# Block-sparse attention and a hard-swish MLP in one kernel: key windows stored as 64 own rows and the next 32, no zero fills, fewer TensorE instructions at the start, a new order

## The chip, the cores and the metric

The kernel runs on one core of a Trainium2 chip. The metric is the device time of one execution in microseconds (us): three runs before the change took 216.30, 216.91 and 217.49 us, so the median is 216.91 us. Engines are named as in the profile: PE (matrix products), DVE (vector), ACT (scalar), POOL (GpSimd, which here issues all loads), SP (which issues stores and small moves).

## The reference

Four batches, eight heads, 768 tokens, head size 64. Each query sees its neighbours at a distance below 16 and, besides, 24 block keys (the maximum over 32 keys each) with the mean of the block's values. The result goes through a two-layer MLP with 2048 hidden units.

```python
k_sum = k.reshape(B, H, nb, 32, D).max(axis=3)
v_sum = v.reshape(B, H, nb, 32, D).mean(axis=3)
mask_l = np.abs(pos[:, None] - pos[None, :]) < 16
scores_all = concat([where(mask_l, scale * q @ k.T, -1e9), scale * q @ k_sum.T + log(32)])
a = softmax(scores_all)
attn = a @ concat([v, v_sum])
h = x @ w_in                      # x: attn, 3072 tokens x 512
out = (h * clip(h + 3, 0, 6) / 6) @ w_out
```

## The kernel before

A tile of 64 queries (QB) needs 96 neighbouring keys (WIN = 64 + 2 x 16) and the 24 block keys, 120 rows in all (KEYS). There are 12 such tiles to a batch. The queries are shifted by 16 against the keys, so that the 96 keys are the 64 own rows of a key tile and 32 rows of a neighbouring one. `kaug[p]` holds the keys of a pair of heads in this form, `vaug[i]` the values of a batch (two buffers, used in turn), `qT` the transposed queries, `at[p]` the exponentials of the scores, `mask` the band.

Before, the 32 foreign rows are those of the tile *before*, and they stand in rows 0 to 31. They are filled by copies (`halo`, `third`) or by an extra load (`load_ahead`). Row 0 of `vaug` up to row 31 is also read by the products that sum values over blocks (`vsum_first`, `vsum`, with `ind` as a 0/1 matrix of 96 rows), and so these rows are first filled with zeros (`empty`, eight operations, one for each buffer and pair of heads).

Work goes in eight half batches s = 0..7 of 384 tokens. For batch 0 the steps are: `k_step` (keys transposed on PE, maximum over blocks on DVE, copies into `kaug`), `q_step` and `q_wide` (queries), `scores`, `vsum_first`, `values_first` (first half, one pair of heads at a time: products, reciprocal, scaling, transposition, copy into x) and `values`. Batches 1 to 3 use `turn`, `scores4`, `vsum`, `values`. Then the MLP: `f1(s, ft)` makes 128 of the 2048 hidden units for 384 tokens (four products of 384 columns, then `relu` on ACT and `gate` on DVE), `f2(s, ts, part)` a quarter of the sum for 128 tokens (four products of 512 columns), and the last quarter is followed by a copy and a store.

The order of everything is written out by hand as a table, `ORDER`: `Plan.issue` takes its tokens from left to right and emits each operation to its engine, and each engine works strictly in that order. `k2.0` is step 0 of `k_step(2)`; `s021` is scores of batch 0, pair 2, half 1; `v01` is `values_first(1)`; `v411` is `values(0, 1, 1)`; `F0x3` is `f1(0, 3)`; `G02x0` is `f2(0, 2, ...)` from column 0. The letter after a colon (A, D) picks ACT or DVE. Loads: `K`, `Q`, `V` for keys, queries, values; `I` and `O` for the two weights; `Q0w` and `Q1w` for rows of queries. Tokens that begin with `~ - _ =` emit products of a tile of ones (`keep`, L774), whose result is never read: `~n` is n products of 512 columns, `-n` of 128, `_n` of 64, `=n` one of n x 64. They stand in front, where PE would else wait for loads.

PSUM has three banks `h`, one `o`, and two pairs `S`; `f1` uses the `h` banks, so three of its results at most wait for ACT and DVE at a time.

Of the kernel before, what the change touches and what calls it, by code (L numbers as in the profile page):

```python
# [9 lines left out]
F32 = mybir.dt.float32  # L10
BF16 = mybir.dt.bfloat16
AF = mybir.ActivationFunctionType
# [17 lines left out]
c.0 K00.0 c.7 c.17 c.6 c.8:A K01.0 c.10:D c.5 c.1 _40 -15 k0.0 k0.2:A c.18 ~1 =2 k1.0 K02.0 ~12 =3 k2.0 k3.0 c.15:D c.2 c.3  # L30
s000.0 k0.3:A c.13:D c.4 c.11:A k1.1 Q00.0 q0.0 k1.4 k0.1 c.20 k1.2:A Q01.0 ~2 =5 q1.0 k0.4 k1.3:D c.9:A c.14:A c.19 k2.3:A
q0.1:A s000.1 q0.2:A =1 s010.0 s010.1 k2.2:A k3.2:D k3.3:D k3.1 V00.0 h000.0:D h001.0:D k2.1 k2.4 s000.2 ~2 =5 v00.0 V01.0 u0.0
h010.0:D s020.0 c.16 s010.2 q1.2:A u0.3:D u0.1:D u0.4:D v01.0 v01.1 v01.2 v00.1 q1.1:A V02.0 h020.0:A h021.0:A h011.0:A v00.2
s020.1 v01.3 v00.3 V03.0 u1.0 u1.3:A h030.0:D s030.0 k3.4 ~2 s030.1 u1.4:D v01.4 h031.0:D Q0w0.0 Q0w1.0 v01.5:D Q0w2.0 =1 q3.0
q3.1:D q2.0 u1.1:A u1.2:D s020.2 v02.0 v02.1 v02.2 s021.0 v02.3 s030.2 v03.0 v03.1 q2.1:A v03.2 s011.0 v03.3 v00.4 v00.5:D
v02.4 s021.1 s011.1 s021.2 v03.4 v03.5:D s011.2 v02.5:A s031.0 s031.1 s001.0 s031.2 I2.0 F0x3.0 F0x3.1 F0x3.2 F0x3.3 F0x3.4
F0x3.5 I4.0 F0x6.0 F0x6.1 F0x6.2 F0x4.0 F0x4.1 F0x4.2 F0x4.3 v411.0 v411.1 F0x5.0 F0x4.4 F0x4.5 v411.2 s001.1 I8.0 u0.2:A
s001.2 F0x8.0 F0x8.1 F0x8.2 F0x5.1 I0.0 F0x5.2 F0x11.0 F0x1.0 F0x11.1 F0x11.2 F0x1.1 F0x1.2 F0x1.3 F0x1.4 F0x1.5 v410.0 v410.1
F0x7.0 F0x7.1 F0x7.2 v410.2 F0x10.0 F0x10.1 I12.0 F0x13.0 F0x13.1 F0x15.0 F0x15.1 F0x13.2 F0x10.2 v411.3 v411.4:D v410.3
v410.4:A F0x15.2 F0x14.0 F0x14.1 F0x14.2 F0x9.0 F0x9.1 F0x9.2 F0x0.0 F0x0.1 F0x2.0 F0x2.1 K13.0 K10.0 c.12:A F0x0.2 K12.0 K11.0  # L40
w10.0 Q1w1.0 F1x14.0 F1x14.1 F1x14.2 F1x4.0 F1x4.1 F1x4.2 F1x2.0 F1x2.1 F1x2.2 w10.1:D F0x2.2 F0x2.3 F0x2.4 F0x12.0 F0x12.1
F0x12.2 F1x8.0 F1x8.1 F1x8.2 F1x1.0 F1x1.1 F1x1.2 F0x0.3 F0x0.4 F0x0.5 F0x2.5 F1x9.0 F1x9.1 F1x9.2 F1x5.0 F1x5.1 F1x5.2 F1x15.0
F1x15.1 w11.0 w11.2 F1x15.2 w11.3:D Q1w4.0 Q1w2.0 Q1w0.0 w10.2 w10.3:D q6.0 q6.1:A q7.0 q7.1:A F1x7.0 F1x7.1 w11.1:A F1x7.2
F1x12.0 F1x12.1 F1x12.2 O0.0 G02x0.0 Q1w5.0 Q1w3.0 q4.0 q4.1:A q5.0 q5.1:A F1x6.0 F1x6.1 F1x6.2 O1.0 G02x0.1 s100.0 s100.1
s100.3 F1x3.0 w12.0 F1x11.0 F1x11.1 w13.0 w13.2 F1x3.1 F1x11.2 w12.2 w12.1:D O2.0 G02x0.2 s101.0 s101.1 O3.0 F1x10.0 G02x0.3
G02x0.4:A w13.3:D w13.1:A s101.3 F1x0.0 G00x0.0 G00x0.1 w12.3:D s100.2 s101.2 s100.4 V10.0 h100.0:D F1x10.1 h110.0:A F1x10.2
F1x3.2 s110.0 s110.1 s110.2 s101.4 s110.3 G00x0.2 G00x0.3 G00x0.4:A V12.0 u4.0 h130.0:D h120.0:A F1x0.1 u4.1:D u4.2:A u4.4:D
u4.3:D u4.5:D G02x0.5 G01x0.0 G01x0.1 G01x0.2 s110.4 F1x0.2 h111.0:A v100.0 v100.1 v100.2 h121.0:A v101.0 v101.1 v101.2 G01x0.3
G01x0.4:A K20.0 K21.0 K22.0 K30.0 K23.0 w21.0 F1x13.0 F1x13.1 F1x13.2 v100.3 v100.4:A w20.0 w21.3 G12x0.0 w21.2:A v101.3
v101.4:A V22.0 H2.0 h101.0:A w20.3 G12x0.1 G12x0.2 F2x2.0 F2x2.1 F2x11.0 F2x2.2 F2x11.1 F2x11.2 s111.0 w23.0 s111.3 F2x1.0  # L50
F2x1.1 F2x1.2 F2x3.0 F2x3.1 F2x3.2 F2x15.0 F2x15.1 F2x15.2 Q22.0 w23.3 G12x0.3 s111.1 G12x0.4:A F2x5.0 F2x5.1 h131.0:A F2x5.2
F2x6.0 G10x0.0 s111.2 w22.0 w22.3 s111.4 w23.4:A V20.0 H2.1:A K33.0 F2x13.0 F2x13.1 F2x13.2 G10x0.1 F2x6.1 F2x0.0 F2x0.1 F2x0.2
u5.0 u5.1:A u5.5:A F2x6.2 v110.0 v111.0 v111.1 v111.2 Q30.0 F2x4.0 F2x4.1 F2x4.2 Q21.0 Q23.0 Q20.0 w22.4:A F2x10.0 F2x10.1
# [12 lines left out]
G30x0.2 F4x13.1 u6.3:A F4x13.2 w33.3 F4x7.0 F4x7.1 F4x7.2 G21x0.5 G20x0.5 v211.4 F4x6.0 F4x6.1 F4x6.2 v211.7 v211.6 v211.5
w30.1 F4x11.0 F4x11.1 F4x11.2 G30x0.3 G30x0.4:A G30x0.5 F4x1.0 F4x1.1 w33.2:A F4x1.2 w32.4:D F4x5.0 F4x5.1 F4x5.2 G22x0.5
s300.0 s300.3 s300.1 F4x3.0 F4x12.0 F4x12.1 F4x9.0 F4x3.1 F4x9.1 w31.5:A w33.4:A w33.1 w32.1 F4x9.2 F4x12.2 w32.5:D s300.2
G31x0.0 G31x0.1 G31x0.2 s300.4 F4x3.2 s310.0 s310.3 s310.4 s310.1 s310.2 F4x0.0 F4x0.1 F4x0.2 F4x10.0 G31x0.3 w30.5:A F4x10.1
w33.5:D F4x10.2 v301.0 v301.1 v300.0 v301.2 v300.1 G31x0.4:A G31x0.5 v300.2 v300.3 v301.3 F5x14.0 F5x14.1 v301.5 v301.7 v301.6  # L70
v301.4 F5x2.0 G42x0.0 G42x0.1 F5x1.0 F5x1.1 F5x2.1 G42x0.2 F5x14.2 F5x1.2 F5x2.2 s301.0 s301.3 G42x0.3 G42x0.4:D s301.1 s301.2
F5x6.0 F5x6.1 F5x6.2 F5x4.0 F5x4.1 F5x4.2 F5x3.0 s311.0 s311.3 s311.4 F5x9.0 F5x9.1 F5x9.2 F5x3.1 F5x3.2 s311.1 s311.2 s301.4
# [90 lines left out]
def kernel(  # L163
# [80 lines left out]
    def low(x):  # L244

        return (1 - x) * HQ
# [563 lines left out]
```

## Time and profile before

| what | value |
| --- | --- |
| median of three runs | 216.91 us |
| span of the profiled execution | 214.9 us (its own time outside the span isn't shown; the median of the runs is 2.0 us above it) |
| PE busy | 208.8 us, 97% of the span, 2564 products |
| DVE busy | 162.7 us, 76% |
| ACT busy | 135.9 us, 63% |
| loads and stores | 22.68 MB, mean 106 GB/s |
| share of the chain that ended last | PE 86%, POOL 5%, DMA 4% |

The page gives averages over a start, a long dense part and an end. The chain of waits is read for where each part is bound, the timeline of each engine for the start, and the table of windows for how full the engines are in each part.

### The profile page before, as it was taken

The page shows a single profiled execution, that of the slowest core. Times are in us where ns is not written, and L with a number is a line of the kernel's source. Part 1 is how long each engine was busy: PE and PEld are TensorE (multiplying, and loading weights), DVE is VectorE, ACT ScalarE, POOL GpSimd, SP SyncE. Part 2 cuts the span into 40 slices and gives each one's busy share as a digit, 9 for nine tenths or more (in the row PEclk, how much of TensorE's full clock was granted, in tenths as well). Part 3 has the DMA queues.
Part 4 walks back from the last instruction along what each step waited for, and adds up shares of the span by engine and source line. Part 5 has one row for each costly group of instructions (what it writes and reads, how often), then busy time and mean ns, then how long its engine had stood idle before and what let it go on. Part 6 is the DMA issues. An engine that isn't in the chain of part 4 may idle for free.

```text
span 214.9 us, 6125 instructions
## 1 busy us (share of the span) xinstructions
PE 208.8 (97%) x2564; PEld 119.7 (56%) x2564; DVE 162.7 (76%) x318; ACT 135.9 (63%) x264; POOL 49.5 (23%) x66
## 2 busy tenths in 40 slices
PE   7998999999999999999999999999999999999994
PEld 7566656555555565565555555555555555564443
DVE  6987999999899999898899889887865555550021
ACT  3987878887898988756578696566346355520110
POOL 7977358906643244000000000000000000000000
PEclk9999999999999999999999999999999999999999
DMA  5999999999999999930334234113314400113123
GB/s 75 159 155 189 203 188 170 190 203 162 206 160 187 181 135 151 108 146 11 38 37 143 28 37 110 49 21 39 70 19 81 78 0 3 49 49 122 52 80 139
DMA packets 91724, 22.68 MB, mean 106 GB/s; under 512 B 82224, under 2 KB 88752, under 8 KB 91696
## 3 DMA queue, kind: packets, MB, share of 16 engines
q0 software_dynamic: 62288, 14.41, 72.7%
q1 hardware_dynamic: 29264, 7.80, 15.4%
q8 instruction: 20, 0.33, 0.6%
q10 hardware_dynamic: 144, 0.07, 0.1%
q14 instruction: 8, 0.07, 0.1%
HBM read 28.82 MB, written 6.29 MB: 163 GB/s over the span
## 4 chain that ended last, share of the span: by engine, by line
PE 86%; POOL 5%; DMA 4%; DVE 1%; ACT 1%; issue 1%; POOLq 0%
PE h L667 38%; PE o L684 33%; PE h L684 5%; DMA qwide<-in_q_dram 4%; PE S L624 3%; PE S L513 3%; POOL vaug L344 2%; PE S L554 1%; ACT vaug L242 1%; POOL first L306 1%; PE S L637 1%; POOL qwide L326 1%; PE S L440 1%; PE S L667 1%; POOL first L313 1%; PE h L582 1%
## 5 line engine op out<-in xcount | busy, mean ns | idle before, releaser
L667 PE MATMUL h<-x,win 128*128 128x384 bf16 x500 | 91.1, 326 | 0.3 <-DVE g L672 0.3
L671 ACT ACTIVATE r<-h 128x384 f32<-128x384 f32 x125 | 58.7, 492 | 38.8 <-PE h L667 36.8
L672 DVE SCALAR_TENSOR_TENSOR g<-r,h 128x384 bf16<-128x384 f32 x125 | 65.7, 546 | 22.7 <-ACT r L671 20.1
L684 PE MATMUL o<-wout,g 128*128 128x512 bf16 x336 | 81.7, 379 | 0.0
L667 PEld LDWEIGHTS <-win 128*128 128x128 bf16 x512 | 48.7, 98 | 35.9 <-issue 0.5
L684 PEld LDWEIGHTS <-g 128*128 128x128 bf16 x416 | 38.7, 98 | 37.4 <-issue 0.3
L521 ACT ACTIVATE at<-S 120x768 bf16<-120x768 f32 x24 | 18.6, 811 | 5.5 <-PE S L513 5.4
L242 ACT COPY ot<-o 128x512 f32<-128x512 f32 x17 | 10.0, 586 | 15.4 <-PE o L684 14.2
L522 DVE TENSOR_TENSOR at<-at,mask 96x768 bf16<-96x768 bf16 x24 | 12.6, 549 | 2.0 <-ACT at L521 1.6
L606 DVE TENSOR_TENSOR xn<-S,rc 128x768 bf16<-128x768 f32 x14 | 13.3, 950 | 0.3
L242 DVE COPY ot<-h 128x512 f32<-128x512 f32 (+1 forms) x3 | 1.6, 555 | 14.3 <-PE h L684 14.3
L344 POOL DMA_DIRECT2D vaug<-in_v_dram x10 | 11.8, 1191 | 0.4 <-DMA first<-in_k_dram 0.2
L684 PE MATMUL h<-wout,g 128*128 128x128 bf16 (+2 forms) x80 | 11.4, 294 | 0.0
L468 DVE TENSOR_REDUCE red<-kaug 128x24 bf16<-128x768 bf16 x12 | 11.2, 942 | 0.1
L242 ACT COPY vaug<-vaug 32x640 bf16<-32x640 bf16 (+3 forms) x17 | 8.9, 574 | 0.8 <-DMA vaug<-in_v_dram 0.5
L242 ACT COPY vaug<-vs 24x1536 bf16<-24x1536 bf16 x6 | 8.8, 1468 | 0.6 <-DVE vs L242 0.5
L456 DVE STREAM_TRANSPOSE kaug<-kraw 128x768 bf16<-128x768 bf16 x8 | 8.1, 1020 | 0.3 <-PE S L513 0.3
L778 PE MATMUL o<-idle 128*128 128x64 bf16 (+2 forms) x70 | 7.0, 278 | 1.1 <-DVE idle L288 1.1
L334 POOL DMA_DIRECT2D kraw<-in_k_dram x8 | 5.9, 737 | 8.9 <-DVE kaug L456 7.3
L513 PEld LDWEIGHTS <-kaug 32*128 32x128 bf16 x576 | 5.3, 92 | 4.4 <-issue 3.6
L643 DVE STREAM_TRANSPOSE y<-xn 128x768 bf16<-128x768 bf16 x8 | 7.6, 964 | 0.2
L624 PEld LDWEIGHTS <-at 120*64 120x64 bf16 x336 | 6.2, 111 | 2.6 <-issue 1.5
(107 smaller groups left out, 183.6 us busy)
## 6 DMA issues: line engine op xcount, KB each, us to landing
out_dram<-ot SPq DMA_DIRECT2D x19, 256.0 KB, 2.3
vaug<-in_v_dram POOLq DMA_DIRECT2D x6, 384.0 KB, 13.1
wout<-in_moe_w_out_dram POOLq DMA_DIRECT2D x4, 512.0 KB, 9.9
win<-in_moe_w_in_dram POOLq DMA_DIRECT2D x3, 512.0 KB, 10.8
kraw<-in_k_dram POOLq DMA_DIRECT2D x8, 192.0 KB, 12.9
x<-y SPq DMA_DIRECT2D x64, 24.0 KB, 2.0
first<-in_k_dram POOLq DMA_DIRECT2D x6, 192.0 KB, 12.3
first<-in_q_dram POOLq DMA_DIRECT2D x6, 192.0 KB, 12.3
```

The source lines that it names most:

```text
L242: {"ACT": nc.scalar.copy, "DVE": nc.vector.tensor_copy, "POOL": nc.gpsimd.tensor_copy}[eng](o, i)
L344: op("POOL", "dma128", lambda: nc.gpsimd.dma_start(out=o[BLK:WIN, a:z, 0:D], in_=rows[:, a:z]), w=[("v", b % 2, c) for c in range(lo, hi)] ...
L468: op("DVE", "max", lambda: nc.vector.tensor_reduce(red.slot[:], w[:, :, BLK:WIN].rearrange("p t (n c) -> p t n c", n=2), axis=AX.X, op=ALU ...
L513: nc.tensor.matmul(X[g // 2].slot[:, g % 2, i * QB:(i + 1) * QB], kaug[2 * u + m][rows, t], qT[rows, 2 * u + m, t * QB:(t + 1) * QB], star ...
L521: op("ACT", "exp", lambda a=a, e=e: nc.scalar.activation(a, X[e].slot[0:KEYS, :, 0:HALF], AF.Exp, scale=scl), r=[X[e]], w=[("at", p, half)])
L522: op("DVE", "masking", lambda m=m: nc.vector.tensor_tensor(m, m, mask[:, low(half):low(half) + HQ].unsqueeze(1).to_broadcast([WIN, 2, HQ, ...
L606: nc.vector.tensor_tensor(o, src[..., 0:D], r.unsqueeze(len(r.shape)).to_broadcast(list(o.shape)), op=ALU.mult)
L624: nc.tensor.matmul(X.slot[64 * c:64 * c + 64, i, m:m + D + 1], a[:, t * QB:(t + 1) * QB], vaug[b % 2][0:KEYS, h, t, 0:D + 1], start=True, ...
L667: nc.tensor.matmul(bank(h)[:, 0:HALF], w_in_sb[:, kt, cols], xt[s].slot[:, kt], start=(kt == 0), stop=(kt == NP - 1))
L671: op("ACT", "relu", lambda: nc.scalar.activation(r.slot[:], bank(h)[:, 0:HALF], AF.Relu, bias=0.5, scale=1.0 / 6.0), r=[h], w=[r])
L672: op("DVE", "gate", lambda: nc.vector.scalar_tensor_tensor(gt[s].slot[:, ft], r.slot[:], 1.0, bank(h)[:, 0:HALF], op0=ALU.min, op1=ALU.mul ...
L684: nc.tensor.matmul(o.slot[:, a:z], gt[s].slot[:, ft, ts * 128:(ts + 1) * 128], w_out_sb[:, ft, a:z], start=(ft == 0), stop=(ft == NFT - 1))
```

## The change

The foreign rows are now the 32 rows of the *next* tile and stand behind the own ones: rows 0 to 63 own, 64 to 95 next. Half 0 of a batch is now its first 384 tokens (`low(x)` is `x * HQ`), and tokens wrap at the end of a batch and no longer at its start. The block sums read only the 64 own rows, so they no longer depend on the foreign rows; `empty` is gone. In `values_first` the products with the block sums cover 128 queries each and are 6 to a pair of heads in place of 12. The table `ORDER` is new from its first to its last row; its products of ones are fewer and wider. Its code:

```diff
 ORDER = """
-c.0 K00.0 c.7 c.17 c.6 c.8:A K01.0 c.10:D c.5 c.1 _40 -15 k0.0 k0.2:A c.18 ~1 =2 k1.0 K02.0 ~12 =3 k2.0 k3.0 c.15:D c.2 c.3
+c.0 K02.0 Q00.0 K01.0 c.5 c.6 K00.0 Q01.0 V01.0 c.1 V00.0 c.11 c.2 ~12 _3 k2.0 V02.0 k2.1 c.9 k2.3:A c.10 c.3 k3.0 q0.0 q0.2:D
+q0.1:A ~1 =2 k1.0 k1.1 k2.2:A ~1 =7 k0.0 k2.4 k1.4 s010.0 k1.3:A s020.0 q1.0 c.12 k1.2:A k0.2:A q1.2:A s010.1 k0.1 k0.3:D
+s010.2 c.8 k0.4 h010.0:D ~4 =4 s000.0 q1.1:A s000.1 k3.2:A k3.1 s000.2 V03.0 v01.0 Q0w0.0 s020.1 k3.3:A h000.0:D u0.0 c.4 v00.0
...
-G70x0.4:D G70x0.5 G60x0.0 G60x0.1 G60x0.2 G72x0.4:D G72x0.5 G60x0.3 G71x256.1 G71x256.2 G60x0.4:D G60x0.5 G71x256.3 G71x256.4
-G71x384.0 G71x384.1 G71x384.2 G71x384.3 G71x384.4:D G71x384.5
+G60x0.0 G70x0.4:A G60x0.1 G60x0.2 G71x384.3 G71x0.0 G72x0.4:A G71x256.0 G72x0.5 G71x0.1 G71x384.4:D G60x0.3 G71x0.2 G70x0.5
+G60x0.4:A G71x256.1 G71x0.3 G71x384.5 G71x0.4:A G71x256.2 G71x256.3 G60x0.5 G71x256.4 G71x0.5
 """
...
-    ind = sb([WIN, NQ, 32], BF16, "ind")
+    ind = sb([QB, NQ, 32], BF16, "ind")
...
-        return (1 - x) * HQ
+        return x * HQ
...
-    def empty(eng, i, c):
-        o = vaug[i][0:BLK, 2 * c:2 * c + 2, :, 0:D].bitcast(F32)
-        if eng == "DVE":
-            nc.vector.memset(o, 0.0)
-        else:
-            nc.scalar.activation(o, idle[0:BLK, 0:1].unsqueeze(1).unsqueeze(1).to_broadcast([BLK, 2, NQ, D // 2]), AF.Copy, scale=0.0)
...
-            out=qnat[:, hs], in_=q[0, hs, HALF - PAD:S - PAD].rearrange("h (p s) d -> p h s d", s=m)),
+            out=qnat[:, hs], in_=q[0, hs, PAD:PAD + HALF].rearrange("h (p s) d -> p h s d", s=m)),
...
-        op("POOL", "dma128", lambda: nc.gpsimd.dma_start(out=o[BLK:WIN, a:z, 0:D], in_=rows[:, a:z]),
+        op("POOL", "dma128", lambda: nc.gpsimd.dma_start(out=o[0:QB, a:z, 0:D], in_=rows[:, a:z]),
...
-            copy(eng, o[0:BLK, hs, a:z, 0:D], o[QB:WIN, hs, a - 1:z - 1, 0:D])
+            copy(eng, o[QB:WIN, hs, a:z, 0:D], o[0:BLK, hs, a + 1:z + 1, 0:D])
...
-                    nc.tensor.matmul(T.slot[lo:lo + BLK, 0:2 * D], ind[:, t], vaug[0][0:WIN, 2 * c:2 * c + 2, t, 0:D],
+                    nc.tensor.matmul(T.slot[lo:lo + BLK, 0:2 * D], ind[:, t], vaug[0][0:QB, 2 * c:2 * c + 2, t, 0:D],
                                      start=(t == 0), stop=(t == NQ - 1))
-        op("PE", "sums2", mms, r=[("v", 0, c) for c in cs] + [("vh", 0, c) for c in cs] + ["ind"], w=[T])
+        op("PE", "sums2", mms, r=[("v", 0, c) for c in cs] + ["ind"], w=[T])
...
-        op("PE", "values1b", lambda: mms(slice(WIN, KEYS), True), r=[("vf", p)], w=[X])
+        def summed():
+            for T in range(3):
+                for h in range(2):
+                    nc.tensor.matmul(bank(X)[:, part(T, h)], at[p][WIN:KEYS, h, 2 * T * QB:(2 * T + 2) * QB], vf[p][WIN:KEYS, h, 0:D + 1],
+                                     start=False, stop=T == 2 and h == 1)
+        op("PE", "values1b", summed, r=[("vf", p)], w=[X])
...
```

What is left out is the same shift carried through the copies, masks and stores. Three places show what the new table moves. The first is POOL, whose instructions from the program's start issue the first loads (`first` holds keys and queries of batch 0) and make `ident`, the matrix that every transposition needs, and `band`. Before:

```order
L306 DMA first<-in_k_dram 96x2x512 x2
L250 MEMSET ident 128x128
L251 ISA
L251 AFFINE_SELECT ident<-ident 128x128
L306 DMA first<-in_k_dram 96x4x512
L255 MEMSET band 96x64
L256 AFFINE_SELECT band<-band 96x64
L258 AFFINE_SELECT band<-band 96x64
L313 DMA first<-in_q_dram 96x4x256 x2
L344 DMA vaug_76<-in_v_dram 64x24x64 x4
```

And with the change:

```order
L295 DMA first<-in_k_dram 96x4x512
L302 DMA first<-in_q_dram 96x4x256
L295 DMA first<-in_k_dram 96x2x512 x2
L302 DMA first<-in_q_dram 96x4x256
L334 DMA vaug_76<-in_v_dram 64x24x64
L249 MEMSET ident 128x128
L250 ISA
L250 AFFINE_SELECT ident<-ident 128x128
L334 DMA vaug_76<-in_v_dram 64x24x64
L254 MEMSET band 96x64
L255 AFFINE_SELECT band<-band 96x64
L257 AFFINE_SELECT band<-band 96x64
```

The double load of keys comes first, and `ident` has moved behind six loads, where it stood behind two.

The second place is DVE at the end of the start, up to the first `gate`: `x_97` is the input of the MLP's first half batch, `qT` the queries of half 1, `at_..` masked exponentials, `g_94` the first gated hidden units. Before:

```order
L242 COPY x_97<-h_90 128x384
L242 COPY qT<-h_92 128x2x384
L242 COPY vaug_76<-vf 24x2x6x64
L599 RECIPROCAL rc_112<-h_90 128x6
L606 TENSOR_TENSOR xn_105<-h_90,rc_112 128x384
L599 RECIPROCAL rc_110<-h_92 128x6
L606 TENSOR_TENSOR xn_103<-h_92,rc_110 128x384
L242 COPY x_97<-o_93 128x384
L498 TENSOR_TENSOR at_74<-at_74,mask 96x2x384
L242 COPY x_97<-h_91 128x384
L498 TENSOR_TENSOR at_73<-at_73,mask 96x2x384
L672 SCALAR_TENSOR_TENSOR g_94<-r_106,h_92 128x384
```

And with the change:

```order
L601 TENSOR_TENSOR xn_103<-h_90,rc_110 128x384
L241 COPY qT<-S_89 128x2x384
L241 COPY vaug_76<-vf 24x2x6x64
L241 COPY qT<-S_88 128x2x384
L241 COPY x_97<-o_93 128x384
L241 COPY x_97<-h_92 128x384
L488 TENSOR_TENSOR at_75<-at_75,mask 96x2x384
L241 COPY vaug_76<-vf 24x2x6x64
L488 TENSOR_TENSOR at_74<-at_74,mask 96x2x384
L488 TENSOR_TENSOR at_73<-at_73,mask 96x2x384
L667 SCALAR_TENSOR_TENSOR g_94<-r_106,h_90 128x384
```

The two reciprocals and scalings of the last pairs now stand ahead of the copy of `qT`, both `qT` copies are on DVE, and no masking stands ahead of the last copy into x.

The third place is POOL again, later: the loads of batch 1's queries (`qraw`), of the second weight and of batch 1's values (`vaug_77`). Before:

```order
L334 DMA kraw<-in_k_dram 32x24x128 x4
L326 DMA qraw<-in_q_dram 128x8x64 x3
L325 DMA qraw<-in_q_dram 16x8x64
L326 DMA qraw<-in_q_dram 112x8x64
L380 DMA wout<-in_moe_w_out_dram 128x4x512
L326 DMA qraw<-in_q_dram 128x8x64 x2
L380 DMA wout<-in_moe_w_out_dram 128x4x512 x3
L344 DMA vaug_77<-in_v_dram 64x48x64 x2
```

And with the change:

```order
L324 DMA kraw<-in_k_dram 32x24x128
L314 DMA qraw<-in_q_dram 112x8x64
L316 DMA qraw<-in_q_dram 16x8x64
L324 DMA kraw<-in_k_dram 32x24x128 x3
L314 DMA qraw<-in_q_dram 128x8x64 x5
L370 DMA wout<-in_moe_w_out_dram 128x4x512 x4
L334 DMA vaug_77<-in_v_dram 64x48x64 x2
```

Two more loads of queries, 128 KB each, stand ahead of the first quarter of the second weight.

200 lines of the change are left out of this document (97 added, 103 removed).

## The prediction

> **What bounds the kernel now.** The page first: PE is at work for 97% of the span. Its products end by a model, so this alone says only that little idle time is seen.
>
> ```profile
> span 214.9 us, 6125 instructions
> PE 208.8 (97%) x2564; PEld 119.7 (56%) x2564; DVE 162.7 (76%) x318; ACT 135.9 (63%) x264; POOL 49.5 (23%) x66
> ```
>
> The windows of 20 us show where the others are full (columns: time with any work, number of instructions, then granted clock, DMA, GB/s).
>
> ```profile
> 0.00:20.00 20.00, 17.83 (x333) 12.22 (x333) 16.47 (x52) 15.21 (x29) 16.90 (x29) 1.00 1.51 140
> ...
> 60.00:80.00 20.00, 19.89 (x292) 11.76 (x291) 18.91 (x32) 17.75 (x35) 7.14 (x10) 1.00 1.97 170
> ...
> 180.00:200.00 20.00, 20.00 (x115) 10.97 (x114) 7.27 (x14) 6.90 (x15) 0.00 (x0) 1.00 0.16 60
> ```
>
> PE is full from 20 us on. DVE is at 95% between 60 and 80 us (18.91 of 20), so an unlucky order there could make PE wait; at the end both have room. Whether PE waits in the dense part is read from the list of waits between 24 and 212 us (in total, times, longest):
>
> ```profile
> PE h L667 <- DVE g L672: 0.3, 1, 0.3
> ...
> PEld L624 <- DVE at L522: 0.8, 2, 0.4
> ...
> PEld L513 <- DVE g L672: 0.4, 1, 0.4
> PEld L513 <- DVE at L522: 0.4, 1, 0.4
> ```
>
> That is 1.9 us at most, part of it beside running products. So a new order can win no more than that after 24 us: the MLP's products there are the same before and after. What is left is the start and the end. The start, from PE's timeline (start, length):
>
> ```profile
> 1.13 3.71 PE L778 MATMUL o<-idle 128*128 128x64 bf16 x55 [1.13 <-DVE idle L288]
> 4.82 0.53 PE L392 MATMUL h<-ident,first 96*64 96x96 bf16 x16
> ...
> 6.45 2.85 PE L778 MATMUL o<-idle 128*128 128x512 bf16 x13
> ...
> 20.31 0.73 PE L442 MATMUL h<-ident,qwide 128*128 128x128 bf16 x10 [0.81 <-DMA qwide<-in_q_dram]
> ...
> 24.17 2.12 PE L667 MATMUL h<-x,win 128*128 128x384 bf16 x12
> ```
>
> The MLP starts at 24.2 us. Until then PE fills time with unread products (L778) and waits 0.81 us for the queries of half 1. What it waits for otherwise is DVE, which prepares keys, values and x from 6.63 to 24.38 us:
>
> ```profile
> 6.63 0.96 DVE L403 TENSOR_REDUCE red<-h 128x24 bf16<-128x768 bf16 x1
> ...
> 10.14 1.55 DVE L242 COPY kaug<-o 128x576 bf16<-128x576 bf16 x4 [0.19 <-PE o L392]
> ...
> 13.22 1.00 DVE L242 COPY vaug<-vaug 32x768 bf16<-32x768 bf16 x3 [0.67 <-DMA vaug<-in_v_dram]
> ...
> 20.75 0.56 DVE L242 COPY qT<-h 128x768 bf16<-128x768 bf16 x1 [0.87 <-PE h L442]
> ...
> 24.03 0.35 DVE L242 COPY x<-h 128x384 bf16<-128x384 bf16 x1
> ```
>
> In these 17.75 us DVE is idle for 0.19 + 0.67 + 0.87 = 1.7 us, so it works for 16.0. The start is bound by DVE, and beside it by the transfers, which bring half 1's queries at 20.3 us.
>
> **The start.** I take DVE's list from the first maximum to the last copy into x, before and after, and price what differs by these groups (count, busy us, mean ns):
>
> ```profile
> L242 DVE COPY vaug<-vaug 32x768 bf16<-32x768 bf16 x5 | 1.8, 352 | 1.5 <-PE S L554 0.8 <-DMA vaug<-in_v_dram 0.7
> ...
> L498 DVE TENSOR_TENSOR at<-at,mask 96x768 bf16<-96x768 bf16 x4 | 2.2, 547 | 0.1
> ...
> L242 DVE COPY vaug<-vf 24x768 bf16<-24x768 bf16 x3 | 1.2, 394 | 0.1
> ...
> L283 DVE MEMSET vaug<- 32x768 f32 x3 | 2.1, 698 | 0.4 <-issue 0.2
> ...
> L285 ACT ACTIVATE vaug<-idle 32x768 f32<-32x768 bf16 x5 | 4.1, 836 | 0.0
> ```
>
> Gone from DVE: the copies of one pair's keys, now ACT's (1.55); two spreads of block sums (2 x 0.39 = 0.78); one masking ahead of the last copy (0.55); one halo of two instructions for one of a single instruction (about 0.4, an estimate from 0.352). New: the second `qT` copy (0.56), one copy of queries (about 0.35, as the copy into x), building the mask and bias, which stood ahead before (about 0.9). Together -3.3 + 1.8 = -1.5 us: 14.5 us of work. ACT can take its share, because the zero fills gave back 4.1 us there (4 of the 5 ahead of 10 us). DVE's own three fills lay ahead of 6.63, where nothing depends on it: worth nothing.
>
> The start of this list is set by POOL and the first keys:
>
> ```profile
> 1.36 1.42 POOL L306 DMA_DIRECT2D first<-in_k_dram  x2 [0.84 <-POOLq L794]
> ...
> 3.31 0.73 POOL L306 DMA_DIRECT2D first<-in_k_dram  x1
> ...
> 4.75 1.33 POOL L313 DMA_DIRECT2D first<-in_q_dram  x2
> 6.07 3.77 POOL L344 DMA_DIRECT2D vaug<-in_v_dram  x4
> ```
>
> `ident` now follows three loads of keys (0.73 + 1.42), two of queries (1.33) and one of values (3.77 / 4 = 0.94): 1.36 + 4.42 = 5.8, and with its own 0.5 (the gap between the first two rows) it is there at 6.3. The keys, first in the queue, are in by then. PE's first transpositions (0.53), at 4.8 before, start at 6.4 and are through at 6.9; DVE starts at 7.05, 0.4 later than before. From there 14.5 us of work end at 21.6 without idle time, at 23.3 with the old 1.7. The other bound: the same bytes (keys, half the queries, values, the other queries) still stand ahead of half 1's queries, so these land at 20.3, or up to 0.5 sooner since the first transfers no longer wait for `ident`. Then transposition (0.5), copy (0.56), spread (0.39), copy (0.56), two copies into x (0.7): 22.5 to 23.0. I take 22.9: **1.5 us earlier** (bounds 1.0 and 2.5). Two groups of scores now stand behind the first MLP product, two MLP products ahead of it: 0.7 - 0.3 = 0.4 given back. **Net -1.1 us** (0 to -2.2).
>
> Hidden, at 0: 24 products with block sums fewer (PE waits there for DVE anyway; without that cover -0.7 at most, from the row below), and the sums over 64 rows (same number, same columns).
>
> ```profile
> 16.02 0.70 PE L582 MATMUL h<-vf,at 24*64 24x65 bf16 x24
> ```
>
>  The 55 first products had 40 x 64 + 15 x 128 = 4480 columns in 3.7 us, the 13 later ones 6336 in 2.85, so the first ran at about half rate (0.83 against 0.45 ns a column), though the clock's column has 1.00 there. The new 15 have 6336: 4.0 to 6.4 us after the clock is taken, so they end between 4 and 6.4, ahead of `ident`: 0 on the path.
>
> [...]
>
> **The dense part.** The finer weave of MLP products can't save more than the 1.9 us of waits. Two of DVE's three copies of foreign keys go to ACT,
>
> ```profile
> L242 DVE COPY kaug<-kaug 128x352 bf16<-128x352 bf16 x3 | 2.3, 754 | 0.0
> ```
>
> 1.5 us less on the engine that PE waited for, so I take half of the waits as gone: **-0.9** (-1.9 to +1.5, since DVE at 95% can lose as much by one late input as it gains by these two). One new wait I can place. The first product with the second weight:
>
> ```profile
> 32.64 0.76 POOL L380 DMA_DIRECT2D wout<-in_moe_w_out_dram  x1 [0.24 <-DMA kraw<-in_k_dram]
> ...
> wout<-in_moe_w_out_dram POOLq DMA_DIRECT2D x1, 512.0 KB, 7.9
> ...
> 44.35 1.03 PE L684 MATMUL o<-wout,g 128*128 128x512 bf16 x4
> 45.30 0.85 PE L440 MATMUL S<-ident,qraw 128*32 128x128 bf16 x48
> ```
>
> Before, it lands at 40.5 and is used at 44.35. Now two more loads of 128 KB stand ahead, 1.7 us at the 154 GB/s that loads of such short rows got:
>
> ```profile
> 14.00:16.00 2.00, 1.79 (x48) 1.36 (x41) 1.83 (x7) 1.49 (x3) 1.46 (x3) 1.00 2.42 154
> ```
>
> So it lands at 42.2. PE comes to it 16 MLP products sooner (16 x 2.12 / 12 = 2.8), a group of transpositions later (0.85) and 1.1 sooner by the start: 41.3. **+0.6** (0 to +1.2), since the transfers may gain half a microsecond too.
>
> **The end.**
>
> ```profile
> 211.40 0.37 ACTq L699 DMA_DIRECT2D out_dram<-ot  x1
> 211.96 0.29 DVE L242 COPY ot<-h 128x128 f32<-128x128 f32 x1 [0.82 <-PE h L684]
> ...
> out_dram<-ot ACTq DMA_DIRECT2D x1, 64.0 KB, 2.1
> ...
> out_dram<-ot SPq DMA_DIRECT2D x1, 64.0 KB, 1.6
> ```
>
> The last small store was SP's (1.6 us); now the last is ACT's piece (2.1), behind ACT's copy of the neighbour: **+0.2** (0 to +0.6).
>
> Sum: -1.1 - 0.9 + 0.6 + 0.2 = **-1.2**: a span of 213.7 for 214.9. The profiled span is 2.0 below the median of 216.9; with the same 2.0 around it the time is 215.7.
>
> **The rivals.**
> - *Transfers take it back* (same): half 1's queries land at 20.3 as before (start -1.0), the second weight's wait is 1.2, the dense part keeps its waits, the end costs 0.2: +0.4, 217.3; with half the waits gone 216.4. I put it at 216.8. For it: the 0.81 us wait, and the weight's 42.2 against 41.3; against it: only these two waits of PE or DVE on a transfer are in the rows above.
> - *PE's clock falls at the start* (slower). Between 5.5 and 9 us PE now has only transpositions and 0.7 us of unread products, where 2.85 us stood. If the clock halves at about 9 us and stays so for as long as at the start (3.4 us) or longer, each of some ten steps between PE and DVE grows by 0.3: +3, less the saving of 1.2: 218.7. It decides as soon as more than 1.2 / 0.3 = 4 steps run at half rate. Against it: PE never idles for more than 0.9 us by my times; for it: the fills were there.
> [...]
> - *All waits go* (faster): DVE's list without idle time (21.6 us: -2.2), the 1.9 us of waits gone, half of them in fact beside products (-1.0), no wait for the weight: -2.2 - 1.0 + 0.2 = -3.0, 213.9.
>
> **How the numbers follow.** Forecast 50%, transfers 18%, clock 15%, all waits 17%. A measurement tells about 0.5% from no change, 1.1 us: faster is below 215.8, slower above 218.0. Of the forecast's own range, 214.8 to 216.4, 36 points lie below 215.8 and 14 above. Faster 36 + 17 = 53; same 14 + 16 = 30; slower 15 + 2 = 17. The range reaches from 213.8 to 217.9: about a tenth is left out on each side.
>
> **What would show it.** The first MLP products of the first half batch in a row at 22.5 to 23 us (right) or at 24 (transfers); 64 x 96 transpositions at 6.4 us; the products of 65 and 128 columns at their old spacing (a doubled spacing between 9 and 20 us is the clock); idle time at L679's first product near 42 us with a transfer of `wout` as its releaser; in the list of waits, fewer of PE's loads waiting for DVE. It is wrong if DVE's last copy into x comes after 23.5, or if waits of more than 2 us show after 24.

## The result, and the profile after

The changed kernel takes 219.03 us (median of six runs, 217.81 to 219.69) against 216.71 us before (six runs, 216.30 to 217.49): the ratio is 1.010, with a 95% interval of 1.0068 to 1.0132. It is slower, by 1.0%. Ratios, here and below, leave out runs that lie more than 1.5% above the fastest of their kernel; where the clock is the question, all runs are listed.

The runs of the changed kernel are of two kinds. Four had the full granted clock on TensorE (1.00 on average): 217.81, 218.27, 218.58 and 219.62 us, so about 218.4 where before has 216.7. Two had less: 219.48 us at 0.984 and 219.69 at 0.977. The profiled run (218.27 us) is one at full clock, so it shows the part of the loss that has nothing to do with the clock. Its page begins

```profile
span 216.6 us, 5945 instructions
PE 207.7 (96%) x2484; PEld 116.9 (54%) x2484; DVE 157.2 (73%) x310; ACT 130.8 (60%) x263; POOL 49.8 (23%) x66
```

The span is 1.7 us longer although PE has 80 products fewer, DVE 5.5 us and ACT 5.1 us less to do. PE's timeline shows the start (start, length, and in brackets how long it was idle before and for whom):

```profile
1.13 4.92 PE L773 MATMUL o<-idle 128*128 128x512 bf16 x15 [1.13 <-DVE idle L279]
6.39 0.87 PE L382 MATMUL h<-ident,first 96*64 96x96 bf16 x32 [0.34 <-POOL ident L250]
...
8.98 0.53 PE L382 MATMUL h<-ident,first 96*64 96x96 bf16 x16 [0.84 <-DMA first<-in_k_dram]
...
21.41 0.83 PE L432 MATMUL S<-ident,qwide 128*128 128x128 bf16 x12
23.12 0.35 PE L480 MATMUL S<-qT,kaug 64*128 64x64 bf16 x12 [0.87 <-DVE qT L241]
...
24.38 0.34 PE L662 MATMUL h<-x,win 128*128 128x384 bf16 x1
24.75 0.35 PE L480 MATMUL S<-qT,kaug 64*128 64x64 bf16 x12
25.03 1.96 PE L662 MATMUL h<-x,win 128*128 128x384 bf16 x11
...
45.16 1.03 PE L679 MATMUL o<-wout,g 128*128 128x512 bf16 x4
```

The first transpositions come at 6.39 us, but the MLP begins at 24.38 and runs on from 25.03, where it ran on from 24.17 before. DVE's timeline and ACT's show where DVE waited between these two points:

```profile
6.96 0.96 DVE L393 TENSOR_REDUCE red<-h 128x24 bf16<-128x768 bf16 x1 [4.63 <-PE h L382]
...
9.56 0.96 DVE L393 TENSOR_REDUCE red<-h 128x24 bf16<-128x768 bf16 x1 [0.75 <-PE h L382]
...
12.43 0.96 DVE L393 TENSOR_REDUCE red<-o 128x24 bf16<-128x768 bf16 x1 [1.46 <-ACT kaug L241]
...
24.23 0.35 DVE L241 COPY x<-h 128x384 bf16<-128x384 bf16 x1
```

```profile
10.55 1.31 ACT L241 COPY kaug<-h 128x480 bf16<-128x480 bf16 x4 [0.69 <-DVE red L393]
```

DVE takes the maximum over a bank of PSUM and ACT copies keys out of the same bank, one after the other in the order of the table; whether the bank or the program's semaphores impose the turn isn't shown. DVE stands idle twice: 0.75 us until pair 1's keys are in (they land at 8.9 us, behind the first queries) and transposed, and 1.46 us until ACT, which had itself waited 0.69 us for DVE's maximum, has copied. How full DVE is between its first maximum and its last copy into x, before:

```profile
6.63:24.38 17.75, 15.42 (x44) 1.00 1.79 179
```

and after, whole and in two pieces:

```profile
6.96:24.58 17.62, 14.75 (x42) 1.00 1.81 180
6.96:13.31 6.35, 4.09 (x11) 1.00 1.91 170
13.31:24.58 11.27, 10.66 (x33) 1.00 1.76 185
```

So DVE's work fell by 0.67 us, but its idle time rose from 2.33 to 2.87, of which 2.26 lie in the first 6.35 us.

From 24 to 212 us the list of waits has these rows for PE and its weight loads, those whose releaser is an engine or a transfer (in total, times, longest):

```profile
PEld L619 <- DVE vaug L241: 0.4, 1, 0.4
...
PE h L662 <- DMA x<-y: 0.4, 1, 0.4
PEld L503 <- ACT r L666: 0.3, 1, 0.3
PEld L619 <- DVE xn L601: 0.3, 1, 0.3
PEld L503 <- ACT x L241: 0.3, 1, 0.3
PEld L619 <- DVE at L512: 0.3, 1, 0.3
PEld L662 <- DVE g L667: 0.3, 1, 0.3
PEld L632 <- DVE xn L601: 0.3, 1, 0.3
...
PE S L480 <- DVE qT L241: 0.2, 1, 0.2
```

That is 2.8 us. The list of before has 2.2: the 1.9 us of waits for DVE that the prediction shows, and this row:

```profile
PEld L554 <- DMA qraw<-in_q_dram: 0.3, 1, 0.3
```

Waits for DVE alone are 1.8 us, where before has 1.9: they hardly fell. Besides, both lists have some 7.5 us of rows for weight loads for which the profile shows no releaser (`issue`). The list doesn't say which waits cost PE time, so the distances between the starts of neighbouring products after 24 us were added up in both traces, which hold the same 928 MLP products (in us; a column's time is about 0.42 ns, as most starts are 216 ns apart behind 512 columns and 162 or 163 behind 384):

```
                                          before   after
MLP product to MLP product, above its
columns' time                               0.91    0.85
MLP product to small one and back,
28 and 29 changes in both, the same         4.66    4.82
value products (65 columns), 328            5.44    6.05
transpositions of scaled values, 31 / 32    1.73    2.08
scores (64 columns), 567 / 597              4.30    4.74
block sums, transpositions of queries       3.17    3.17
```

The finer weave costs next to nothing: the MLP's own products are as dense as before, and PE changes between them and small ones equally often (0.16 us more in all). The loss is 1.5 us and lies almost wholly in three rows. Scores: 30 products that stood ahead of 24 us stand behind it now (0.44). Value products and the transpositions behind them: 0.96 us, of which 0.86 in four places, where the after trace has gaps of 0.18 (61.5 us), 0.28 (64.2), 0.28 (72.9) and 0.12 (93.3) and before has none above 0.1 us. PE waits there in the middle of a small group: for DVE at 61.5, 64.2 and 93.3 us; for the gap at 72.9 us the profile shows no releaser.

### The profile page after: what moved, and what is told of

Its sections match the earlier page's. It is cut to its first block, busy times and chain, and to the rows that moved or that the text cites. A ratio compares the mean times of both kernels' runs of the same rounds, so it can differ in the third digit from the quotient of the medians.

```text
span 216.6 us, 5945 instructions
## 1 busy us (share of the span) xinstructions
PE 207.7 (96%) x2484; PEld 116.9 (54%) x2484; DVE 157.2 (73%) x310; ACT 130.8 (60%) x263; POOL 49.8 (23%) x66
## 4 chain that ended last, share of the span: by engine, by line
PE 77%; DVE 9%; SPq 5%; DMA 4%; ACT 2%; issue 1%; POOL 1%; POOLq 0%
PE h L662 36%; PE o L679 28%; SPq L644 5%; PE h L679 5%; DMA first<-in_k_dram 3%; DVE vaug L241 3%; PE S L619 2%; PE S L503 2%; DVE xn L601 2%; DVE red L393 1%; PE S L662 1%; DMA x<-y 1%; ACT kaug L241 1%; PE S L632 1%; DVE at L512 1%
## 5 line engine op out<-in xcount | busy, mean ns | idle before, releaser
L662 PE MATMUL h<-x,win 128*128 128x384 bf16 x500 | 92.9, 326 | 0.4 <-DMA x<-y 0.4
L679 PE MATMUL h<-wout,g 128*128 128x512 bf16 (+2 forms) x80 | 10.9, 294 | 0.0
L241 ACT COPY kaug<-h 128x480 bf16<-128x480 bf16 (+3 forms) x12 | 4.2, 415 | 7.0 <-DVE red L393 7.0
L619 PE MATMUL S<-vaug,at 120*64 120x65 bf16 x336 | 7.5, 196 | 0.1
L241 ACT COPY vaug<-vs 24x1536 bf16<-24x1536 bf16 x5 | 7.3, 1468 | 0.1
L241 ACT COPY ot<-h 128x512 f32<-128x512 f32 (+1 forms) x3 | 1.4, 517 | 9.3 <-PE h L679 9.3
## 6 DMA issues: line engine op xcount, KB each, us to landing
wout<-in_moe_w_out_dram POOLq DMA_DIRECT2D x4, 512.0 KB, 10.7
```

Source lines behind the costliest of these rows:

```text
L241: {"ACT": nc.scalar.copy, "DVE": nc.vector.tensor_copy, "POOL": nc.gpsimd.tensor_copy}[eng](o, i)
L619: nc.tensor.matmul(X.slot[64 * c:64 * c + 64, i, m:m + D + 1], a[:, t * QB:(t + 1) * QB], vaug[b % 2][0:KEYS, h, t, 0:D + 1], start=True, ...
L662: nc.tensor.matmul(bank(h)[:, 0:HALF], w_in_sb[:, kt, cols], xt[s].slot[:, kt], start=(kt == 0), stop=(kt == NP - 1))
L679: nc.tensor.matmul(o.slot[:, a:z], gt[s].slot[:, ft, ts * 128:(ts + 1) * 128], w_out_sb[:, ft, a:z], start=(ft == 0), stop=(ft == NFT - 1))
```

## The experiments

All 15 kernels were timed beside runs of the kernel before on the same chip, whose median was 216.7 to 217.0 us. There were four such sets, on three chips, so kernels of different sets are best compared by their ratios to before. In its 88 runs in these sets the clock of before was below 0.998 in five, each time 0.992.

**The order of before on the changed code.** The new `ORDER` goes, the old one stays, without the tokens of the zero fills; constants and loads are renumbered as the new code needs it.

```diff
-c.0 K02.0 Q00.0 K01.0 c.5 c.6 K00.0 Q01.0 V01.0 c.1 V00.0 c.11 c.2 ~12 _3 k2.0 V02.0 k2.1 c.9 k2.3:A c.10 c.3 k3.0 q0.0 q0.2:D
+c.0 K00.0 c.7 c.9 c.6 K01.0 c.5 c.1 _40 -15 k0.0 k0.2:A c.10 ~1 =2 k1.0 K02.0 ~12 =3 k2.0 k3.0 c.2 c.3 s000.0 k0.3:A c.4 k1.1
...
```

> The changed code (own rows first, no zero fills, block sums over 64 rows, 6 wide products with block sums) issued in the order of before, with the products of ones of before. Theory A, the new order is what loses: this is not slower than before, 215.7 to 216.9 us, since DVE's three and ACT's five zero fills are gone and nothing is added. Rival B, the new layout itself loses (own rows in partitions 0 to 63, wide products): about 218.5 to 219 us, as the changed kernel.

Measured: 218.68 us (216.51 to 226.5, 12 runs), ratio 1.0031 (0.9998 to 1.0065). The median hides two kinds of runs. Four at full clock: 216.51, 216.55, 216.93, 217.16, in the median 216.74, which is 0.3 less than before's 217.02 beside it. Eight with less: 218.0 to 218.71 at 0.992, 219.51 at 0.984, and on to 226.5 at 0.953. What follows: at full clock the code alone loses nothing, as theory A said, and yet without any new order it already loses the clock in eight runs of twelve; that the median lies where rival B put it comes from the clock, which neither named.

**Half of the order each.** The table is cut at `w10.0`, the first transposition of batch 1's keys: the new order in front of it and the old one behind, and the other way round.

> The changed code; the new order up to the first turn of batch 1, the order of before from there. In the traces the changed kernel has about 0.7 us more of PE's work left at 40 us than before, and 1.65 us more at 150 us. If the loss of the start is carried to the end and the dense part of the new order adds the rest: 0.7 us over before, 217.4 (217.0 to 217.8). If the start's loss is made up later where the order of before is used: 216.7.

> The changed code; the order of before up to the first turn of batch 1, the new order from there. If the new order's dense part loses by itself: about 1.0 us over the time of the kernel that has the old order throughout, 217.0 to 217.8. If the dense part only suffers from the late start: the same as that kernel, within 0.3 us.

Measured: new front 219.63 us (219.5 to 219.77, four runs, all at 0.992), ratio 1.0123 (1.0108 to 1.0137); old front 218.79 us (217.78 to 220.54), 1.0093 (1.0058 to 1.0127), with only two runs of six at full clock. The old front with the new rest is 1.5 us above the old order throughout at full clock (218.22 and 218.33 against 216.74); the new front with the old rest has no run at full clock, so its own price can't be read here. Both forecasts were too low. The profiled run of the new front shows what the clock does. Its windows (busy time of PE, its loads, DVE, ACT and POOL; then granted clock, DMA share, GB/s):

```profile
17.49:20.90 3.41, 2.78 (x77) 2.21 (x73) 3.19 (x12) 2.90 (x6) 3.10 (x5) 1.00 1.36 205
20.90:24.31 3.41, 3.20 (x46) 2.65 (x44) 3.31 (x8) 3.03 (x6) 1.42 (x3) 0.50 1.30 201
24.31:27.73 3.42, 3.42 (x64) 2.14 (x63) 3.33 (x8) 3.26 (x6) 1.47 (x3) 1.00 1.32 207
```

For 3.41 us, in the middle of the start, PE runs at half its clock (0.50). In the 3.41 us ahead of this PE was at work for 2.78 us and idle for 0.63 in all, with 77 products (36 ns each in the mean, where the starts of products of 512 columns are mostly 216 ns apart). In the profiled run of the change it was at work for 2.98 us in the same window, and the clock stayed at 1.00. What makes the clock fall isn't shown by this. (The ends of products are modelled, so how much of these 2.78 us the array was really fed isn't shown.)

**The maximum ahead of ACT's copies.** In the bank of pair 0, `k0.1` (maximum, DVE) goes ahead of `k0.2` (ACT).

```diff
-k1.2:A k0.2:A q1.2:A s010.1 k0.1 k0.3:D
+k1.2:A k0.1 k0.2:A q1.2:A s010.1 k0.3:D
```

> The changed kernel with one operation moved: the maximum over the blocks of pair 0's keys (DVE) stands ahead of ACT's copy from the same PSUM bank, not behind it. In the trace DVE sat idle for 1.46 us there, released by ACT's copy. If the two readers of one bank take turns in the table's order and this turn is on the path: the maximum starts at 11.0 and not at 12.4 us, the MLP starts 0.5 to 1.4 us earlier, and the time is 0.5 to 1.4 us below the changed kernel's. Rival: the loads set the start, and nothing is gained (within 0.3 us).

Measured: 218.09 us (217.54 to 218.61), 1.0048 (1.0030 to 1.0066); three runs at full clock (217.54 to 218.03), three at 0.983 to 0.992. At full clock that looks like 0.7 us gained (medians 217.71 and 218.4), but by three runs against four; it is repeated below with the clock held.

**The clock held by fills.** Unread products of 512 columns (0.22 us each: most starts of such products are 216 ns apart in the traces of before and of the change) are put where PE waits anyway: eight in the old order (one narrow one goes; the expectation says seven), twelve in the new one. Nothing else differs from the first experiment and from the change.

```diff
-V01.0 u0.0
+V01.0 ~1 u0.0
...
-Q0w2.0 =1 q3.0
+Q0w2.0 ~4 q3.0
```

```diff
-~4 =4 s000.0 q1.1:A s000.1
+~4 =4 ~1 s000.0 q1.1:A ~3 s000.1
...
-u1.4:D s031.0
+u1.4:D ~4 s031.0
```

> The changed code in the order of before, as in the first experiment, with 7 more unread products of 512 columns between 13 and 23 us, where PE waits. In the first experiment the runs with a granted clock of 1.0 took 216.5 to 217.2 us and those with 0.95 to 0.992 took 218 to 226.5, and its profile shows the clock halved from 19.6 to 23.0 us. If PE's thin work at the start is what lets the clock fall: nearly all runs at 1.0 and 216.3 to 217.0 us. Rival, the clock falls by the chip's own reasons: the same spread as without the fills, a median near 218.7.

> The changed kernel, its order kept, with 12 more unread products of 512 columns at the places between 13 and 22 us where PE waits. If the clock's fall is only part of the loss: no run below a clock of 0.995, and 217.8 to 218.6 us, as the runs of the changed kernel at full clock; what is left over before is then the new order's own waits. If the clock is all of it: 216.9 or less. If the fills themselves get in the way: over 219.

Measured: old order, filled: 217.39 us (216.86 to 218.1), 1.0022 (1.0006 to 1.0038). New order, filled: 217.88 us (217.05 to 218.41), 1.0033 (1.0016 to 1.0051). In both, all twelve runs have a clock of 0.998 or more. With 1.7 us of products whose results nobody reads, the old order on the changed code is 1.3 us shorter in the median than without them, and its longest run falls from 226.5 to 218.1. That this order loses the clock without the fills (eight runs of twelve) and keeps it with them (none of twelve below 0.998) is shown. (In the mixed tables further down, which have these fills too, one run of seven and one of nine fell to 0.992.) The new order is then 1.0 us above before, and 0.5 above the old order. Without fills the distance between the two orders at full clock was 1.7 us (218.4 and 216.74): the fills make the old order 0.65 us longer, the new one not. Which of the two distances is the price of the order isn't settled.

**Fills taken out of before.** The counter-test on the kernel before: its unread products behind the transpositions of pair 2 go, at five places of which two are shown.

```diff
-Q01.0 ~2 =5 q1.0
+Q01.0 q1.0
...
-Q0w2.0 =1 q3.0
+Q0w2.0 q3.0
```

> The kernel before without its unread products behind pair 2's transpositions (7 of 512 columns and a few smaller ones, from 10.9 to 19.2 us). If these hold the clock: most runs fall below 0.995 and take 218 to 220 us. If they only pass the time: 216.9 us as before, at full clock.

Measured: 217.87 us (215.41 to 223.42, 10 runs). Five at full clock, 215.41 to 216.37 us, about 1.1 shorter than before with its fills (medians 215.81 and 216.89); five from 219.37 (0.976) to 223.42 (0.962). Windows of its profiled run, one of the latter:

```profile
9.75:13.16 3.41, 1.73 (x50) 1.21 (x50) 2.85 (x9) 2.49 (x7) 2.38 (x4) 1.00 2.24 163
13.17:30.23 17.06, 16.98 (x291) 12.38 (x292) 11.19 (x31) 10.60 (x18) 10.11 (x13) 0.50 1.67 188
```

Half clock (0.50) for 17.06 us, five times the 3.41 us above, during which PE looks full (16.98 of 17.06 us) although no work was added. So the fills of before cost about a microsecond and are worth it. The ratio, 0.9943 (0.9917 to 0.9969), is made of the five runs at full clock and can't be had reliably.

**Fewer fills.** The old order with about 0.6 us of fills at three places (`=4`, 256 columns, ahead of `v01.1` and `v00.1`; `~2` in place of `=1` ahead of `q3.0`).

> The changed code in the order of before, with 3 added unread products where 7 stood in the filled kernel (two of 256 columns ahead of the products with block sums, one of 512 and the rest of an old one where PE waits for half 1's queries). If a thin 3.4 us stretch of PE lets the clock fall and a little work is enough to hold it: all runs at a clock of 0.995 or more and 216.4 to 217.0 us, not slower than before. If it is too little: some runs at 0.992 and below, 218 us or more.

Measured: 217.89 us (216.64 to 225.51). Seven of twelve at full clock (six of them 216.64 to 217.17), five from 220.91 to 225.51 (0.985 to 0.968). Too little.

**Keys ahead of queries.** To take away DVE's idle 0.75 us: pair 1's and pair 0's keys are loaded ahead of the first queries, and `k1` stands ahead of `q0` on PE and DVE; `k0.1` goes ahead of `k0.2` as well. One of the places:

```diff
-c.0 K02.0 Q00.0 K01.0 c.5 c.6 K00.0 Q01.0
+c.0 K02.0 K01.0 c.5 c.6 K00.0 Q00.0 Q01.0
```

> The changed kernel with its start reordered: all loads of keys ahead of the loads of queries, pair 1's keys ahead of the first queries on PE and DVE, and pair 0's maximum ahead of ACT's copy from the same bank. In the trace of the changed kernel PE waited until 8.98 us for pair 1's keys and DVE was idle for 0.75 and 1.46 us there. If these two waits set the start: the MLP starts 0.8 to 1.5 us earlier and full-clock runs take 217.0 to 217.6. If moving the maximum alone gave all there is: 217.5 to 218.0.

Measured: 219.49 us (219.04 to 220.1), 1.0111 (1.0087 to 1.0135). It gains nothing: the one run at full clock is its fastest (219.04), within those of the change (217.81 to 219.62). In the profiled run PE waits 1.64 us for the first queries, up to 9.83 us, and the clock is at half (0.50) from 10.7 to 17.4 us. The wait moved from the keys to the queries; what it costs without the loss of clock isn't shown.

**The maximum first, at full clock.** The filled new order with `k0.1` ahead of `k0.2`.

> The changed kernel with the 12 added unread products of the filled one, and pair 0's maximum ahead of ACT's copy from the same bank. The filled kernel took 217.9 us at full clock. If the turn of DVE behind ACT is on the path at the start: 217.3 to 217.6. If not: 217.9 within 0.2.

Measured: 218.07 us (217.64 to 218.75, all at 0.999 or 1.000), 1.0054 (1.0034 to 1.0074): no gain on 217.88. The timeline shows DVE's third maximum 1.5 us sooner and the last copy into x 0.15 us sooner than in the filled order without the move (12.39 and 24.23 us):

```profile
10.91 0.90 DVE L393 TENSOR_REDUCE red<-o 128x24 bf16<-128x768 bf16 x1
...
24.08 0.35 DVE L241 COPY x<-h 128x384 bf16<-128x384 bf16 x1
```

The 1.46 us of idle time was real, but what follows waits for something else as well: DVE's fourth maximum is only 0.68 us sooner (it waits 0.29 us for ACT's copy), its first reciprocal 0.38 (it waits 0.33 us for PE). So this wait was hardly on the path to the MLP.

**Halves again, filled.** The old front with the new rest, and the new front with the old rest, both with the fills of their front.

> The changed code; the order of before with its added unread products up to the first turn of batch 1, the new order from there; the clock should stay full. The whole of the old order, filled, took 217.4, the whole of the new one, filled, 217.9. If the new order's dense part loses by itself what its trace shows after 60 us (1.0 us): 218.2 to 218.6. If its loss came from the late start alone: 217.4 within 0.3.

> The changed code; the new order with its added unread products up to the first turn of batch 1, the order of before from there. If the new start is late by the 0.7 to 0.9 us seen in the traces and this is carried to the end: 217.9 to 218.3. If the order of before takes it up in its own waits between 38 and 60 us: 217.4 within 0.3.

Measured: 218.52 us (217.38 to 220.46), 1.0083 (1.0047 to 1.0119), and 218.03 us (217.55 to 219.32), 1.0057 (1.0037 to 1.0076). Both fall into the forecasts for a loss by the new dense part (218.2 to 218.6) and for a late new start carried to the end (217.9 to 218.3). But together they would put the whole new order some 1.8 us above 217.39, and it is 0.5 above (217.88). By their ratios (1.0083 and 1.0057 beside 1.0022 for old and old, 1.0033 for new and new) the old front with the new rest looks longer than both pure tables, though its interval just touches that of new and new (1.0047 and 1.0051); the other is not clearly longer than new and new. The halves don't add up, so this pair gives no price for either; that each table was made for its own seam would explain it, but wasn't tried.

**DVE's waits at 61 to 64 us.** Three edits of the filled new order: one group of four MLP products goes ahead of batch 1's value products; one masking goes behind the spreads of block sums on DVE; both.

```diff
-F1x0.2 v100.0 u4.5:A v100.1 v101.0 v100.2 v101.1 G01x0.2 G01x0.3
+F1x0.2 G01x0.2 v100.0 u4.5:A v100.1 v101.0 v100.2 v101.1 G01x0.3
```

```diff
-h100.0:D s110.4 h110.0:D
+h100.0:D h110.0:D
...
-u4.5:A v100.1
+u4.5:A s110.4 v100.1
```

> The new order with fills in the start (217.88 us, ratio 1.0033) and one group of four 512-column products (G01x0.2, 0.85 us) moved from behind to ahead of batch 1's first value products (v100.0). Theory A, the dense part's loss sits at 60 to 65 us, where PE waits for DVE's spreads of block sums: PE has the group to do while DVE finishes, 0.4 us shorter, but it then comes 0.85 us sooner to the transpositions that wait for DVE's scaling, so about 0.2 to 0.4 us in all: 217.5 to 217.7. Theory B, the loss is spread evenly over the finer weave (entries into small groups): no change, 217.9.

> The new order with fills, and on DVE one masking of exponentials (s110.4, 0.56 us, read only much later) moved from ahead of batch 1's spreads of block sums to behind them. Theory A (the loss sits at 60 to 65 us and DVE's list sets it there): spreads, value products, reciprocal, scaling and transpositions all come 0.56 us sooner, so 0.4 to 0.6 us shorter: 217.3 to 217.5. Theory B (spread evenly over the weave): no change, 217.9.

> Both moves together. Theory A: the wait of 0.43 us at the first value products is gone and that at the transpositions at most what it was, 0.6 to 1.0 us shorter than 217.88: 216.9 to 217.3. Theory B: 217.9.

Measured: 218.08 us (1.0033 to 1.0073), 218.48 us (1.0044 to 1.0097), 218.12 us (1.0037 to 1.0075), all at 0.998 or more. None gains. PE's timeline around 62 us, with the order unchanged, with the group moved, with the masking moved, and with both:

```profile
61.66 1.27 PE L619 MATMUL S<-vaug,at 120*64 120x65 bf16 x48 [0.43 <-DVE vaug L241]
...
64.61 1.12 PE L632 MATMUL S<-ident,xn 128*128 128x128 bf16 x12
```

```profile
61.87 0.95 PE L619 MATMUL S<-vaug,at 120*64 120x65 bf16 x48
...
64.89 0.51 PE L632 MATMUL S<-ident,xn 128*128 128x128 bf16 x6 [0.62 <-DVE xn L601]
```

```profile
62.45 0.54 PE L619 MATMUL S<-vaug,at 120*64 120x65 bf16 x22 [0.83 <-DVE at L512]
```

```profile
62.70 0.54 PE L619 MATMUL S<-vaug,at 120*64 120x65 bf16 x22 [0.30 <-DVE at L512]
...
64.97 0.51 PE L632 MATMUL S<-ident,xn 128*128 128x128 bf16 x6 [0.42 <-DVE xn L601]
```

With the group moved, the wait at the value products goes and comes back at the transpositions behind them. The other two edits didn't do what was meant: the moved masking is not read much later, as expected of it, but by the second group of value products (`v101`), which now waits for it (0.83 and 0.30 us). Theory A, as put, falls: the last six transpositions start at 64.9 to 65.0 us in the three, 0.2 to 0.3 sooner than with the order unchanged (65.22), but the block sums ahead of all the edits were already 0.15 to 0.39 sooner, and no median is below 217.88.

The traces show one thing that these edits left as it was. Between the block sums and the last six transpositions before has 24 MLP products for PE,

```profile
58.22 2.76 PE L684 MATMUL o<-wout,g 128*128 128x512 bf16 x12
...
61.97 1.04 PE L684 MATMUL o<-wout,g 128*128 128x512 bf16 x4
62.84 0.81 PE L667 MATMUL h<-x,win 128*128 128x384 bf16 x4
...
63.83 1.03 PE L684 MATMUL o<-wout,g 128*128 128x512 bf16 x4
```

and the change has 16:

```profile
59.25 1.90 PE L679 MATMUL o<-wout,g 128*128 128x512 bf16 x8
...
62.20 1.90 PE L679 MATMUL o<-wout,g 128*128 128x512 bf16 x8
```

DVE is not slower there: from the start of the block sums to the end of the second scaling it is 6.0 us after (58.47 to 64.49) and 6.7 before (57.43 to 64.08). So the new order leaves PE less to do while DVE works, and moving a group of four within the 16 only chooses where PE waits. Whether more products in this stretch would win the 0.46 us of its two gaps back wasn't tried.

No version beats before reliably. The nearest with the clock held are the old order filled (1.0022) and the new order filled (1.0033).

## Why the prediction was wrong

It said 215.7 us, within 213.8 to 217.9, and faster; it is 219.03 and slower. Both signs that it had named for being wrong came: DVE's last copy into x after 23.5 us (24.23), and waits of more than 2 us after 24 (2.8, though before has 2.2 if every row is counted).

- **Start, -1.1 us: this step failed.** The first half of it held. `ident` came after the six loads, PE's first transpositions at 6.39 (6.4 said), DVE's first maximum at 6.96 (7.05 said); the fills in front cost nothing; half 1's queries were in when PE came to them at 21.41. DVE's work was 14.75 us (14.5 said). But the saving of 1.5 was counted from 16.0 us, which was the stretch less only those three idle times that a row named; the windows give 15.42, so it was 0.67. And idle time was bounded at 0 to 1.7 us; it was 2.87, with two new waits in it: DVE and ACT now read the same banks in turn, and pair 1's keys land behind the first queries. But with the larger of these waits gone the last copy into x came only 0.15 us sooner, so naming them doesn't say which chain sets the end of the start; that stays open. The last copy into x ends at 24.58 where 22.9 was said for the end of this work. The 0.4 us for the scores moved behind the first MLP products was right (0.44).
- **Clock, a rival at 15%, came true in part of the runs.** Its place was the start, though later than the 9 us said (in five profiled runs of the experiments the half clock began between 10.7 and 20.9 us). The 3.4 us at the start, which it took from before, are in the trace, from the products' starts: 0.83 ns a column from 1.13 to 4.5 us, and 0.43 right behind. With the change this rate lasts from 1.13 to 5.4 us; the clock's column has 1.00 there in both. The rival's time is near by luck (218.7 said; 219.5 and 219.7 in the two runs of the change with less clock): it was added up as 3 us for the clock on a kernel 1.2 us faster, and those two runs are 1.1 to 1.3 us above the full-clock ones of a kernel 1.7 us slower. The argument against it, that PE never idles for more than 0.9 us, was wrong: in the new front with the old rest, the clock fell after 3.41 us in which PE worked for 2.78. That the fills were there, given for it, was the better one, and the test without fills shows it (five runs of ten at 0.961 to 0.984). By the full-clock runs the clock is not the whole cause: those are about 1.7 us above before as well.
- **Dense part, -0.9 us: this step failed too.** It took half of the waits as gone because DVE has less to copy. Waits for DVE stayed (1.9 and 1.8 us), all named waits rose from 2.2 to 2.8, and small groups of products took 0.96 us more, mostly in four gaps that before doesn't have, three of them waits for DVE. DVE's work from 24 to 212 us fell by 0.9 us (142.9 to 142.0), but where PE waits depends on what the order gives it to do meanwhile: at 58 to 65 us 16 MLP products in place of 24. That a finer order might lose by one late input was priced (up to +1.5) and not taken. The bound itself, that no order can win more than the named waits, was too strong: the distances between products show time that no row names.
- **Second weight, +0.6 us:** no wait came. The load landed at 42.1 us (42.2 said), but PE reached the first product with it at 45.16 us, not at 41.3. It comes to it 4 MLP products sooner in the new table (25 groups of four stand ahead, 26 before), not the 16 that were counted, and the start brought nothing. **End, +0.2:** 0; from the start of the last product to the end both take 3.2 us.

Sum at full clock: first MLP product 0.2 later, scores 0.44, small groups 0.96, together 1.6; the span grew by 1.7. That says where the time went; no experiment won any of it back, so its cause is read from the traces and not shown. The median of the runs grew by 2.3; the rest goes with the two runs at less clock and with one of 219.62 us at full clock that nothing here explains.

## What to carry to other kernels

Unread products in a thin start are no waste until the runs, not one profile, show that the clock stays up without them: look at the granted clock of every run, and don't take PE's busy time for a sign that it holds (here it fell behind 3.41 us with PE at work for 2.78, and eight more products of 512 columns, 1.7 us, kept it at 0.998 or more in all twelve runs of the old order). When work goes from one engine to another, look at the turns that both then take at the same buffer, and test whether they are on the path: here the longest was 1.46 us and worth 0.15. In a new order count, between handing work to another engine and needing it back, how many products PE still has. And subtract work from a window's busy time, never from a span less the waits that happen to have a row.

## What was not expected of the hardware

In the profiled runs the granted clock is at half for 3.41 us (the new front with the old rest, the old order on the changed code), for some 6.7 us (the maximum moved, keys ahead of queries) or for 17.06 us (before without its fills), about one, two and five times 3.41, though PE is busy by the profile for much of the 3.41 us ahead of it (2.78, 2.85 and 1.73 us in the new front, the old order and before without its fills), and the same kernel does it in some runs and not in others: five of ten runs of the kernel before without its fills, and, with the fills of before, eight of twelve of the old order on the changed code. One stretch costs 1.3 to 2.0 us in the latter (216.7 at full clock, 218.0 to 218.7 at 0.992); at 0.953 it was 9.8. It isn't a fixed price: with the maximum moved it was 0.4 us (217.71 in the median at full clock, 218.16 in the one run at 0.992), and of the old front with the new rest the run of 217.78 at 0.992 is the fastest. What exactly counts as work enough was not settled: the changed code lost the clock in the order of before, and the sums over 64 rows in place of 96 and the missing 24 products, which differ there, were not tried apart.
